# Dense and memory matmuls issued as four column tiles, and a planner that keeps GpSimd and SBUF-only DVE operations apart

## The chip, the cores and the metric

One core of one Trainium2 chip runs the whole program. The metric is device time in microseconds (us), the median of repeated executions. A profiled execution gives a trace beside it: every instruction of every engine with its start and length. The engines are PE (TensorE, matmuls; the trace lists its weight loads apart, as PEld), DVE (VectorE), ACT (ScalarE), POOL (GpSimd) and SP, which only issues DMAs here.

## What is computed

Two layers of the same kind follow each other, on 2048 tokens of 640 features, in bf16. A layer adds an attention block and then a feed-forward block to `x`, each behind a layer norm. Cut to what matters:

```python
H, Dh, N, L = 32, 20, 4, 512              # heads, width of a head, segments, tokens of a segment
def attention(x):                         # x: (1, 2048, 640)
    q, k, v = x @ wq, x @ wk, x @ wv      # split into heads and segments
    for s in range(N):
        p = softmax(q_s k_s^T * Dh**-0.5 + causal mask)
        a_dot = p v_s
        pq = phi(q_s)                     # phi(t) = t + 1 if t > 0 else exp(t)
        a_mem = (pq M) / (pq z + 1e-6)    # what the memory holds of the segments before
        o_s = g * a_mem + (1 - g) * a_dot # g = sigmoid(beta), one per head
        M, z = M + phi(k_s)^T v_s, z + sum(phi(k_s))
    return concat(o) @ wo
def feed_forward(x):
    return relu(x @ w1) @ w2              # 1728 hidden features
for layer in range(2):                    # the same weights twice
    x = x + attention(norm(x)); x = x + feed_forward(norm(x))
```

## The kernel before

**Tiling.** Work goes by layer `a` (0, 1) and segment `s` (0 to 3) of 512 tokens. The features lie in five chunks of 128 partitions. PE does these kinds of work, and the form in which it uses its array of 128 x 128 is what the change is about:

- *Dense* products, in `group` (L644 to L656): the first matmul of a group is recorded at L651, the others at L654. Query, key and first feed-forward products stream 512 columns, value, output and second feed-forward products 320. Each uses the whole array (128 rows by 128 columns).
- *Scores* (`scores`, L1114): a head is only 20 wide, so four heads sit in four strips of 32 rows and run side by side (row tiles). Keys and queries are brought into that layout by way of DRAM (`spill`, `fill`). A pair of head groups has five rounds; a round fills PSUM slots X and Y, and ACT turns each into exponentials (`exps`, L1166). There are 32 pairs, so 160 rounds. POOL zeroes what the causal mask forbids (`causal`, L1178).
- *Values* (`apply`, L1257): exponentials times values. The output of a head is 21 wide, so four heads sit in four strips of 32 columns (column tiles); 16 matmuls of 512, 384, 256 and 128 columns for one group of heads. Pairs 2 and 3 go another way, `values_by_token` (L1208): the whole array, 40 short matmuls of 21 columns at a time.
- *Memory* reads (`mem_read`, L1007) and writes (`mem_write`, L1058): the whole array, 84 to 168 columns each.
- The last 64 hidden features of the feed-forward block (`ffn_last`, L1405): two strips of 64 columns.
- Idle matmuls (`keep_busy`, L638) that the planner puts into gaps of PE.

**The order** of all instructions is worked out on the host by a planner, `Sched`. Each piece of the work is a generator (a *stream* with a priority) that yields operations (`Op`); an operation has the engines that may do it, a price in ns, the waits, and a `mode`, the form of PE: "full", "rows" or "cols". At each step the planner takes, over all streams, the operation that could start first, ties going to the lower priority. Where an operation's mode is not the one that PE is in, `switch` is added to its price (L264) and 97 ns to the time kept for it (L336). A "cols" operation that would come while PE is in "full" is held back by up to 4 us while scores remain (`JOIN_NS`, L297), so that it rather follows scores. DVE operations are priced at 66 ns plus their columns, and nothing is known to the planner of what POOL does at that time. 48 plans are made with 48 values of `switch`; the one that a replay with random DMA delays (`late`) finds shortest is emitted. The waits in the program come from the data alone, not from the planner's times.

Of the kernel before, what the change touches and what calls it, by code (L numbers as in the profile page):

```python
# [11 lines left out]
D = 640  # L12
# [101 lines left out]
class Op:  # L114
# [4 lines left out]
    def __init__(self, alts, waits, dma=None, acq=None, urgent=False, take=(), mode="full"):  # L119
        self.alts = alts  # L120
        self.mode = mode
# [4 lines left out]
        self.take = take  # L126

# [38 lines left out]
IDLE_NS = 300.0  # L166
SURE_NS = 800.0
# [9 lines left out]
class Sched:  # L177


    def __init__(self, prog, switch):  # L180
        self.P = prog
        self.switch = switch
        self.log = []
        self.free = {e: 800.0 for e in ENGS}
        self.t = {}
        self.events = {}
        self.streams = []
        self.dma_free = 0.0
        self.pe_mode = "full"
        self.spare = []  # L190
        self.idle_fn = None

    def keep_busy(self, op, start):
# [10 lines left out]
        if n > 1:  # L204
            self.log.append(("pe", 56.0 * n, 0.0, s.tks, [], False))
# [47 lines left out]

    def _alts(self, op):
# [7 lines left out]
        for k, (e, hold, fns, tail) in enumerate(op.alts):  # L262
            m = PE_MARGIN if e == "pe" else 0.0
            if e == "pe" and op.mode != self.pe_mode:  # L264
                hold = hold + self.switch
            start = max([self.at(t) + SEM_NS + m for t in waits], default=0.0)
            start = max(self.free[e], start)
            res.append((start + hold, start, k, e))
        return res

    def run(self):
        while True:
# [52 lines left out]
            e, hold, fns, tail = op.alts[k]  # L325
            waits, slot = op.waits, None
# [7 lines left out]
            if e == "pe":  # L334
                self.keep_busy(op, start)
                if op.mode != self.pe_mode:  # L336
                    hold = hold + SWITCH_NS
            self.P.waits(e, waits)
            self.free[e] = end
            if e == "pe":  # L340
                self.pe_mode = op.mode
# [15 lines left out]
            self.log.append((e, hold, tail, waits, out if isinstance(out, list) else [out], op.dma is not None))  # L357
            st[2], st[3] = None, ((slot, out) if slot is not None else out,)

    def late(self, seed):  # L360
# [5 lines left out]
        for e, hold, tail, waits, out, is_dma in self.log:  # L366
# [3 lines left out]
            if e == 'pe' and start - free[e] > 800.0 and start > 10e3:  # L370
                start += COOL_NS
            free[e] = start + hold
# [15 lines left out]
def pe(ns, fns, waits=(), acq=None, take=(), mode="full"):  # L388
    return Op([("pe", ns, fns, 190.0)], waits, acq=acq, take=take, mode=mode)
# [29 lines left out]
def plan(switch, sb, sem_, psum, dram, A_x, A_wq, A_wk, A_wv, A_wo, A_beta, B_x, B_w1, B_w2, out):  # L419
# [156 lines left out]
    def consts():  # L576
# [37 lines left out]
        ta = yield dve(32, 1, lambda e: e.tensor_scalar(gt[:, 1, :], gt[:, 0, :], 1.0, None, ALU.add), [te])  # L614
        tr = yield dve(256, 1, lambda e: e.reciprocal(gt[:, 1, :], gt[:, 1, :]), [ta])
        tg = yield dve(32, 1, lambda e: e.tensor_scalar(gt[:, 2, :], gt[:, 1, :], -1.0, 1.0, ALU.mult, ALU.add), [tr])
# [5 lines left out]
        for c in range(FC):  # L622
            h0, h1 = CH_H0[c], CH_H1[c]
            mc = maskg[:, CH_OFF[c]:CH_OFF[c + 1]].rearrange("p (h e) -> p h e", e=DH + 1)[:, :, 0:DH]
            tm = yield dve(140, 1, lambda e, mc=mc, h0=h0, h1=h1: e.tensor_tensor(
# [18 lines left out]
    def group(slots, n, mms, waits):  # L644

        bk = tk = None
        last = len(mms) - 1
        for k, (a, b, *w) in enumerate(mms):
            w = list(w[0]) if w else []
            if k == 0:  # L650
                bk, tk = yield pe(mm_ns(n), [(lambda e, bk, a=a, b=b: e.matmul(  # L651
                    bk.ap[:, 0:n] if len(b.shape) == 2 else bk.ap[:, 0:n].rearrange("p (i n) -> p i n", n=128), a, b, start=True, stop=(last == 0)), last == 0)], list(waits) + w, acq=slots)
            else:
                tk = yield pe(mm_ns(n), [(lambda e, k=k, a=a, b=b, bk=bk: e.matmul(  # L654
                    bk.ap[:, 0:n] if len(b.shape) == 2 else bk.ap[:, 0:n].rearrange("p (i n) -> p i n", n=128), a, b, start=False, stop=(k == last)), k == last)], w)
# [3 lines left out]
    def stats(t, xt):  # L659
        tk = None  # L660
        for c2 in range(2):
# [3 lines left out]
            mv[:, t, :], stats6[:, t, :, :].rearrange("p c s -> p (c s)")), [tk])  # L665
        return tk

    def chain(t0, n, tk, sq=None):

        sl = slice(t0, t0 + n)  # L670
        if sq is None:
            tk = yield dve(n, 1, lambda e: e.tensor_scalar(lnU[:, sl], mv[:, sl, 1], LN_EPS, None, ALU.add), tk)  # L672
        else:
            tk = yield dve(n, 1, lambda e: e.tensor_scalar(lnU[:, sl], sq, 1.0 / D, LN_EPS, ALU.mult, ALU.add), tk)
# [11 lines left out]
    def lnorm(s, x_tks, pool_, parts=1):  # L686
# [3 lines left out]
        for p0 in range(0, 4, n):  # L690
# [11 lines left out]
            for i in range(p0, p0 + n, 2):  # L702
# [4 lines left out]
                bx, t0 = yield dve(D, 4, lambda e, bx, t=t: nm(e, bx, t, 0), [tch], extra=120, acq=XN)  # L707
                t1 = yield dve(D, 4, lambda e, bx=bx, t=t: nm(e, bx, t, 1), [tch], extra=120)
# [6 lines left out]
    def normed(t, k, bx, tch):  # L715
        return dve(D, 4, lambda e: e.tensor_scalar(  # L716
# [236 lines left out]
    def phi_(n):  # L953
        def f(a, s):
# [6 lines left out]
            for c in range(FC):  # L961
# [5 lines left out]
                tr = yield dve(512, 4, lambda e, rt=rt, q=q: e.tensor_scalar(  # L967
# [7 lines left out]
                tp = yield dve(512, 2, lambda e, rt=rt, dst=dst: e.tensor_tensor(dst, dst, rt.ap, ALU.min),  # L975
# [18 lines left out]
    def mem_read(hb):  # L994
        def f(a, s):
# [8 lines left out]
            for i in range(NJ):  # L1004
                fns = []
                for z, (c, h0, h1) in enumerate(lst):
                    fns.append((lambda e, bk, c=c, h0=h0, h1=h1, z=z, i=i: e.matmul(  # L1007
                        bk.ap[:, (h0 - 16 * hb) * 21:(h1 - 16 * hb) * 21],
                        STGS[sx(a, s)][:, c, 1, i * 128:(i + 1) * 128],
                        BD[:, CH_OFF[c] + (h0 - CH_H0[c]) * 21:CH_OFF[c] + (h1 - CH_H0[c]) * 21],  # L1010
                        start=(z == 0), stop=True, skip_group_check=True), z == len(lst) - 1))
# [565 lines left out]
```

## Time and profile before

| | |
|---|---|
| median of 3 runs | 562.56 us (562.47 to 562.56) |
| the profiled execution | 562.46 us |
| its span, first to last instruction | 560.6 us |
| instructions in the trace | 12651, of them 5110 matmuls and 5111 weight loads |
| scores, first to last start | 19.47 to 478.80 us |

The profile names an instruction by its line in the kernel, so that L651 and L654 together are all dense products. Busy time of PE counts a matmul from its start to a modelled end; two that follow each other overlap, so the pace of PE is read from the starts. Rows of the table of windows give, for a stretch of the span, each engine's busy time and count of instructions.

### The profile page before, as it was taken

The numbers are of one execution on the slowest core, as the hardware profiler recorded it, in microseconds if no ns is written. First come the engines' busy times: TensorE is split into PE (matmuls) and PEld (weight loads), VectorE is DVE, ScalarE is ACT, GpSimd is POOL, SyncE is SP. The second block draws the span as 40 slices with busy tenths as digits, with TensorE's granted clock in tenths as the row PEclk, the third lists the DMA queues.
The fourth block names the chain that finished last, engine by engine and source line by source line (L and its number), as shares of the span: only waits on it lengthen the run. The fifth ranks groups of instructions, "written<-read, shape, count | busy, mean of one in ns | idle before, by whom it ended". The sixth has DMA issues, their size and how long they took to land.

```text
span 560.6 us, 12651 instructions
## 1 busy us (share of the span) xinstructions
PE 555.5 (99%) x5110; PEld 302.6 (54%) x5111; DVE 410.8 (73%) x1060; ACT 409.7 (73%) x522; POOL 194.3 (35%) x302
## 2 busy tenths in 40 slices
PE   8999999999999999999999999999999999999998
PEld 7654545545644455645356554465445654665655
DVE  5898899776998787877888987889824866651202
ACT  5799999987699779787897789877856788323140
POOL 4534344333354444344433443335401433100000
DMA  8599988741374137443373505550325510422101
GB/s 269 118 201 219 254 202 164 172 123 44 90 175 99 50 89 185 88 99 79 97 179 52 127 20 137 131 120 20 67 77 154 114 43 20 93 69 55 41 1 47
DMA packets 132219, 61.43 MB, mean 110 GB/s; under 512 B 111042, under 2 KB 122050, under 8 KB 132162
## 3 DMA queue, kind: packets, MB, share of 16 engines
q1 hardware_dynamic: 131942, 60.37, 45.7%
q8 instruction: 40, 0.66, 0.5%
q10 hardware_dynamic: 220, 0.26, 0.2%
q14 instruction: 17, 0.14, 0.1%
HBM read 20.57 MB, written 12.85 MB: 60 GB/s over the span
## 4 chain that ended last, share of the span: by engine, by line
PE 90%; DVE 8%; DMA 1%; ACT 0%; POOL 0%; issue 0%
PE ps L654 58%; PE ps L651 12%; PE ps L1114 9%; PE ps L1257 7%; DVE stats L662 2%; PE ps L1058 2%; PE ps L1007 2%; DVE x_sb L1328 1%; PE ps L1405 1%; DVE stg L827 1%; DMA x_sb<-in_A_x_dram 1%; DVE xn_tok L704 1%; DVE av L1265 0%; DVE xn_tok L716 0%; DVE mv L664 0%; ACT PT L1166 0%
## 5 line engine op out<-in xcount | busy, mean ns | idle before, releaser
L1166 ACT ACTIVATE PT<-ps 128x1024 bf16<-128x1024 f32 x320 | 310.1, 1022 | 66.1 <-PE ps L1114 64.5
L1178 POOL TENSOR_SCALAR_AFFINE_SELECT PT<-PT 128x512 bf16<-128x512 bf16 x256 | 166.3, 668 | 267.7 <-ACT PT L1166 267.7
L654 PE MATMUL ps<-w_r,hT 128*128 128x320 bf16 (+2 forms) x768 | 123.4, 299 | 0.1
L654 PE MATMUL ps<-xnT,w_r 128*128 128x512 bf16 x416 | 113.6, 379 | 0.0
L1328 DVE TENSOR_TENSOR x_sb<-x_sb,ps 128x320 bf16<-128x320 bf16 (+1 forms) x128 | 60.4, 479 | 70.2 <-PE ps L654 69.9
L654 PEld LDWEIGHTS ps<-w_r,hT 128*128 128x128 bf16 x768 | 72.2, 98 | 34.2 <-issue 6.3
L1436 ACT ACTIVATE hT<-ps 128x512 bf16<-128x512 f32 x55 | 33.0, 599 | 46.4 <-PE ps L654 46.1
L1114 PE MATMUL ps<-pad 20*128 20x384 bf16 (+3 forms) x1024 | 64.9, 301 | 0.0
L654 PEld LDWEIGHTS ps<-xnT,w_r 128*128 128x128 bf16 x416 | 39.7, 98 | 42.1 <-issue 2.9
L662 DVE BATCH_NORM_STATS2 stats<-x_sb 128x6 f32<-128x320 bf16 x126 | 55.9, 470 | 2.3 <-DMA x_sb<-in_A_x_dram 2.0
L1265 DVE CAST av<-ps 128x512 bf16<-128x512 f32 x56 | 38.3, 684 | 12.9 <-PE ps L1257 12.5
L1114 PEld LDWEIGHTS ps<-pad 20*128 20x128 bf16 x1024 | 18.2, 92 | 51.4 <-ACT PT L1166 24.2
L654 PE MATMUL ps<-wo_r,oT 128*128 128x320 bf16 x256 | 45.3, 299 | 0.0
L1434 DVE TENSOR_SCALAR hT<-ps 128x512 bf16<-128x512 f32 x49 | 33.5, 684 | 10.5 <-PE ps L654 10.0
L1257 PE MATMUL ps<-PT,v_aug 128*32 128x256 bf16 (+5 forms) x896 | 40.7, 302 | 0.0
L651 PE MATMUL ps<-xnT,w_r 128*128 128x512 bf16 x104 | 39.6, 381 | 0.0
L654 PE MATMUL ps<-wv_r,xnT 128*128 128x320 bf16 x192 | 35.8, 300 | 0.0
L654 PE MATMUL ps<-xnT,wk_r 128*128 128x512 bf16 (+1 forms) x140 | 35.5, 349 | 0.0
L676 POOL TENSOR_TENSOR rstd<-lnU,mhalf 128x2 f32<-128x2 f32 (+2 forms) x25 | 20.3, 811 | 39.9 <-DVE lnU L672 39.7
L654 PE MATMUL ps<-xnT,wq_r 128*128 128x512 bf16 (+1 forms) x140 | 33.9, 349 | 0.0
L1301 DVE TENSOR_TENSOR o_sb<-avt,rden 128x320 bf16<-128x320 bf16 x60 | 33.3, 572 | 0.7
L654 PEld LDWEIGHTS ps<-wo_r,oT 128*128 128x128 bf16 x256 | 24.8, 98 | 11.3 <-issue 1.3
(120 smaller groups left out, 686.9 us busy)
## 6 DMA issues: line engine op xcount, KB each, us to landing
pad<-scr SPq DMA_DIRECT2D x124, 80.0 KB
scr<-stg SPq DMA_DIRECT2D x34, 256.0 KB, 2.9
out_dram<-x_sb SPq DMA_DIRECT2D x15, 160.0 KB, 1.8
w_r<-in_B_w_dram SPq DMA_DIRECT2D x10, 216.0 KB, 3.3
w_r<-in_B_w_dram SPq DMA_DIRECT2D x13, 160.0 KB, 2.7
x_sb<-in_A_x_dram SPq DMA_DIRECT2D x9, 160.0 KB, 3.3
scr<-w_r SPq DMA_DIRECT2D x5, 256.0 KB, 3.5
x_sb<-in_A_x_dram SPq DMA_DIRECT2D x3, 320.0 KB, 7.3
```

The costliest lines, as they stand in the source:

```text
L651: bk, tk = yield pe(mm_ns(n), [(lambda e, bk, a=a, b=b: e.matmul(bk.ap[:, 0:n] if len(b.shape) == 2 else bk.ap[:, 0:n].rearrange("p (i n) ...
L654: tk = yield pe(mm_ns(n), [(lambda e, k=k, a=a, b=b, bk=bk: e.matmul(bk.ap[:, 0:n] if len(b.shape) == 2 else bk.ap[:, 0:n].rearrange("p (i ...
L662: tk = yield dve(320, 1, lambda e, c2=c2: e.bn_stats(stats6[:, t, c2, :], x_sb[:, t, c2 * 320:(c2 + 1) * 320]), xt)
L1114: fns.append([(lambda e, z=z, j=j, hh=hh, N=N, o=o, sl=sl: e.matmul(ps[:, hh, o:o + N], sl.ap[32 * hh:32 * hh + DH, z, 0, 128 * j:128 * j ...
L1166: tx = yield act(1024, lambda e, dst=dst, src=src: e.activation(dst, src, ACT.Exp, scale=SCALE), sc + pw)
L1178: tm = yield pool(600.0, lambda e, reg=reg: e.affine_select(out=reg, in_=reg, pattern=[[0, 4], [1, 128]], compare_op=ALU.is_ge, fill=0.0, ...
L1257: fns.append((lambda e, bk, j=j, hh=hh, pt=pt, g=g0 + z: e.matmul(bk.ap[32 * hh:32 * hh + wide(g, hh), 128 * j:L], VAUG[vx(a, s)][:, j].re ...
L1265: te = yield evac(L, 1, lambda e, sl=sl, z=z, bk=bk: e.tensor_copy(sl.ap[:, z], bk.ap), lambda e, sl=sl, z=z, bk=bk: e.activation(sl.ap[:, ...
L1301: to = yield dve(320, 1, lambda e, dst=dst, src=src, rz=rz: e.tensor_tensor(dst, src, rz, ALU.mult), [tg] + OSB.tks)
L1328: ta = yield dve(n, 1, lambda e: e.tensor_tensor(x_sb[:, t, c0:c0 + n], x_sb[:, t, c0:c0 + n], bk.ap[:, 0:n], ALU.add), [tk] + list(waits) ...
L1434: th = yield evac(512, 1, lambda e, dc=dc, bk=bk: e.tensor_scalar(hT[:, dc, :], bk.ap[:, :], 0.0, None, ALU.max), lambda e, dc=dc, bk=bk: ...
L1436: lambda e, dc=dc, bk=bk: e.activation(hT[:, dc, :], bk.ap[:, :], ACT.Relu), [tk] + HT.tks)
```

## The change

**Column tiles.** `pe` gets `cols`, a second list of instructions, and `cols_ns`, what they take more. `group`, `mem_read` and `mem_write` hand over such a list: each matmul of 128 output columns becomes four, with 32 columns of the weights each, that write partitions 0 to 31, 32 to 63, 64 to 95 and 96 to 127 of the same PSUM bank. The planner takes the list when PE is in "cols" or "rows" and scores remain (`mode_of`); PE is then in "cols". Behind an operation in "full" that has no such list (L1208 above all) dense work stays in "full" until the next scores, and after the last scores all of it is in "full". `ffn_last` goes from two strips of 64 columns to four of 32.

**POOL and DVE.** Operations of DVE that read and write SBUF alone, with the exception of bn_stats and a few others, are marked `shared` (`dvs` in place of `dve`), as is every POOL operation. In the planner and in its replay, one that would start while a shared operation of the other engine runs starts 140 ns before that one's end instead. No wait is added to the program. Two prices change: the mask from 600 to 635 ns, bn_aggr by +40 ns.

The diff, cut to its core:

```diff
+OTHER = {"dve": "pool", "pool": "dve"}
+OVER_NS = 140.0
...
+    def mode_of(self, op):
+        return "cols" if op.cols is not None and self.pe_mode in ("cols", "rows") and not self.streams[0][4] else op.mode
...
-            if e == "pe" and op.mode != self.pe_mode:
+            if e == "pe" and self.mode_of(op) != self.pe_mode:
                 hold = hold + self.switch
+            if e == "pe" and op.cols is not None and self.mode_of(op) != op.mode:
+                hold = hold + op.cols_ns
             start = max([self.at(t) + SEM_NS + m for t in waits], default=0.0)
             start = max(self.free[e], start)
+            if op.shared and e in OTHER:
+                a, b = self.spans[OTHER[e]]
+                if a <= start < b - OVER_NS:
+                    start = b - OVER_NS
...
+            mode = self.mode_of(op)
+            if e == "pe" and mode != op.mode:
+                fns = op.cols
...
+def dvs(n, mode, fn, waits=(), extra=0.0, acq=None, urgent=False):
+
+    op = dve(n, mode, fn, waits, extra, acq, urgent)
+    op.shared = True
+    return op
...
+            def whole(e, bk, k=k, a=a, b=b, wide=wide):
+                return e.matmul(to(bk.ap, wide), a, b, start=(k == 0), stop=(k == last))
+
+            def tile(e, bk, y, k=k, a=a, b=b, wide=wide):
+                return e.matmul(to(bk.ap[32 * y:32 * y + 32], wide), a[:, 32 * y:32 * y + 32], b,
+                                start=(k == 0), stop=(k == last))
...
-                bk, tk = yield pe(60.0 * len(lst), fns, phi + bdt, acq=MISC[:1])
+                bk, tk = yield pe(60.0 * len(lst), fns, phi + bdt, acq=MISC[:1], cols=cols, cols_ns=3.0 * len(lst))
...
-                tm = yield pool(600.0, lambda e, reg=reg: e.affine_select(
+                tm = yield pool(635.0, lambda e, reg=reg: e.affine_select(
...
             for z in range(2):
-                fns.append((lambda e, bk, k=k, z=z: e.matmul(
-                    bk.ap[64 * z:64 * z + 64, 0:256].rearrange("p (i n) -> p i n", n=128),
-                    w1_r[:, k, NFULL * 128:DFF], feat(xt, k)[:, 2 * z:2 * z + 2],
-                    start=(k == 0), stop=(k == FC - 1)), k == FC - 1 and z == 1))
+                for y in range(2):
+                    fns.append((lambda e, bk, k=k, z=z, y=y: e.matmul(
+                        bk.ap[64 * z + 32 * y:64 * z + 32 * y + 32, 0:256].rearrange("p (i n) -> p i n", n=128),
+                        w1_r[:, k, NFULL * 128 + 32 * y:NFULL * 128 + 32 * y + 32], feat(xt, k)[:, 2 * z:2 * z + 2],
+                        start=(k == 0), stop=(k == FC - 1)), k == FC - 1 and (z, y) == (1, 1)))
```

More of the change, by code (lines that the diff above doesn't have):

```diff
@@ L126, in __init__ @@
         self.take = take
+        self.shared = alts[0][0] == "pool"
 class Slot:
@@ L335, in run @@
                 self.keep_busy(op, start)
-                if op.mode != self.pe_mode:
+                if mode != self.pe_mode:
                     hold = hold + SWITCH_NS
+                if mode != op.mode:
+                    hold = hold + op.cols_ns
+            shared = op.shared and e in OTHER
+            if shared:
+                self.spans[e] = (start, end)
             self.P.waits(e, waits)
@@ L365, in late @@
         dma_free = 0.0
-        for e, hold, tail, waits, out, is_dma in self.log:
+        spans = {"pool": (0.0, 0.0), "dve": (0.0, 0.0)}
+        for e, hold, tail, waits, out, is_dma, shared in self.log:
             m = SEM_NS + (PE_MARGIN if e == "pe" else 0.0)
```

99 lines of the change are left out of this document (62 added, 37 removed).

## The prediction

> **What bounds the kernel now.** I read the page's engine totals first, then the chain that ended last.
>
> ```profile
> span 560.6 us, 12651 instructions
> PE 555.5 (99%) x5110; PEld 302.6 (54%) x5111; DVE 410.8 (73%) x1060; ACT 409.7 (73%) x522; POOL 194.3 (35%) x302
> ...
> PE 90%; DVE 8%; DMA 1%; ACT 0%; POOL 0%; issue 0%
> ```
>
> PE is busy from end to end and is 90% of the chain: it is the bound. The question is whether PE's time is all arithmetic. The table of windows, cut at the first scores, the end of the weight loads and the last scores, has three stretches behind the start (columns: window, length, then busy us and count of PE, PEld, DVE, ACT, POOL).
>
> ```profile
> 19.50:106.00 86.50, 85.96 (x909) 46.66 (x909) 80.05 (x225) 81.53 (x109) 36.52 (x54) 1.00 0.87 196
> 106.00:479.00 373.00, 372.91 (x3511) 193.12 (x3509) 294.86 (x741) 299.25 (x362) 145.41 (x221) 1.00 0.42 97
> 479.00:560.60 81.60, 79.23 (x542) 48.05 (x535) 23.88 (x58) 18.83 (x31) 2.88 (x5) 1.00 0.20 51
> ```
>
> In the middle 373 us PE is busy for 372.91, while ACT (299.25) and DVE (294.86) have a fifth of their time free: what PE saves there shortens the kernel. Between 19.5 and 106 ACT is busy 81.53 of 86.5 us and DVE 80.05, so little can be saved there. The clock column (third from the right) is 1.00 throughout.
>
> But "busy" hides something, and PE's timeline shows it (start, length to the last matmul's end, line, tile, shape of the first, count).
>
> ```profile
> 200.70 0.40 PE L1114 MATMUL ps<-pad 20*128 20x384 bf16 x8
> 201.02 0.73 PE L1257 MATMUL ps<-PT,v_aug 128*32 128x512 bf16 x16
> 201.68 0.31 PE L651 MATMUL ps<-wo_r,oT 128*128 128x320 bf16 x1
> 201.83 0.30 PE L654 MATMUL ps<-wo_r,oT 128*128 128x320 bf16 x1
> 201.97 0.33 PE L1007 MATMUL ps<-BD,stg 128*128 128x84 bf16 x3
> 202.14 0.84 PE L654 MATMUL ps<-wo_r,oT 128*128 128x320 bf16 x5
> 202.82 0.30 PE L651 MATMUL ps<-wo_r,oT 128*128 128x320 bf16 x1
> 202.95 0.57 PE L654 MATMUL ps<-wo_r,oT 128*128 128x320 bf16 x3
> 203.46 0.40 PE L1114 MATMUL ps<-pad 20*128 20x256 bf16 x8
> ```
>
> Matmuls overlap, so I go by starts. Five dense matmuls of 320 columns take 202.14 to 202.82: 0.136 us each, 0.425 ns a column. Scores (L1114) run four side by side: 384 + 128 columns are 0.218 us, but the next start comes after 0.32. Values (L1257) are 1280 columns, 0.544 us, and the next start comes after 0.66. Three dense ones should take 0.408 and the scores come after 0.51. So each change between scores (row tiles), values (column tiles) and dense work (whole array) costs 0.10 to 0.12 us with no arithmetic in it; the first matmul behind it is late too (201.68 to 201.83, 0.15 for 0.136).
>
> **How many changes.** Going down PE's rows of the timeline I count 163 stretches of scores; the first and the last:
>
> ```profile
> 19.47 0.40 PE L1114 MATMUL ps<-pad 20*128 20x512 bf16 x4
> ...
> 478.80 0.40 PE L1114 MATMUL ps<-pad 20*128 20x384 bf16 x8
> ```
>
> From 106 to 479 us there are 315 changes of form: 128 into scores (124 from dense, 4 from column work), 48 scores to values, 79 scores to dense, 52 column work to dense, 8 dense to column work. There are 80 before and 7 after.
>
> **The change, part by part.** (1) Behind scores and values, a dense or memory matmul is issued as four of 32 output columns each, in the values' form. The 52 + 8 changes between values and dense work go; scores still cost one change in and one out. An edge out of column work costs 0.116 + 0.014, one into it 0.10 + 0.014: 52 × 0.130 + 8 × 0.114 = **-7.7 us** in the middle window. The last feed-forward block (L1405) goes from two tiles of 64 to four of 32, because those two forms cost a change as well:
>
> ```profile
> 393.11 0.74 PE L1405 MATMUL ps<-xnT,w_r 128*64 128x256 bf16 x10
> 393.77 0.73 PE L1257 MATMUL ps<-PT,v_aug 128*32 128x512 bf16 x16
> 394.43 0.34 PE L1007 MATMUL ps<-BD,stg 128*128 128x147 bf16 x3
> ```
>
> 1280 columns again, 0.544, and 0.66 to the next start. It happens once: counted in the margin.
>
> (2) Leaving four column tiles for scores costs 0.116 where leaving dense work cost 0.10: the four start one behind the other. 124 such exits at 0.013: **+1.6 us**.
>
> (3) Dense in steady state. Inside a values visit four tiles run 512 + 384 + 256 + 128 columns at the dense rate, so I price the dense matmuls (L651 and L654, the window's rows by line below) at nothing: 245 + 1,353 = 1,598. One of 320 columns now needs eight instructions in 0.136 us, 17 ns each.
>
> ```profile
> 106.00:479.00 373.00, 82.67 (x245) 23.68 (x244) 1.00 0.42 97
> 106.00:479.00 373.00, 275.51 (x1353) 126.64 (x1353) 1.00 0.42 97
> ...
> 201.02 0.40 PE L1257 MATMUL ps<-PT,v_aug 128*32 128x512 bf16 x4
> ...
> 201.02 0.12 PEld L1257 LDWEIGHTS ps<-PT,v_aug 128*32 128x32 bf16 x8 [0.21 <-issue]
> ...
> 55.07 1.16 PE L1208 MATMUL ps<-w_r,PT 128*128 128x21 bf16 x40
> ```
>
> The four 512-column matmuls of a values visit are done in 0.40 us, and forty load-and-matmul pairs of L1208 start within about 1.0 us (1.16 less the length of the last), 25 ns a pair, 12.5 ns an instruction: fast enough, though for 80 instructions and not thousands. That pace is the cover; what it costs if it is missing is rival C.
>
> (4) Memory matmuls (L1007, L1058) are short: 84 to 168 columns by the code, and the three from 201.97 to 202.14 above took 0.057 us each. The window's rows by line (L1007, then L1058):
>
> ```profile
> 106.00:479.00 373.00, 13.50 (x120) 8.78 (x120) 1.00 0.42 97
> 106.00:479.00 373.00, 7.41 (x88) 5.94 (x87) 1.00 0.42 97
> ```
>
> That is 208. From above: the shortest step from four tiles to the next four is that from 256 columns to 128, 256 × 0.425 = 0.109 us, so the four loads could take up to 0.109 unseen, 0.052 more than 0.057. From below: nothing. The nearest row is that of the eight loads above: all within 0.12 us although one takes 0.097 (the median by the view of that line, below), so they start 3 ns apart and run side by side. I take 4 ns: **+0.8 us**.
>
> ```profile
> L1257 PEld LDWEIGHTS ps<-PT,v_aug x896: 87/97/98, 82.0 to 483.6; 128*32 128x32 bf16 x173, 128*21 128x21 bf16 x7
> ```
>
> (5) Before 106 us nine changes go (7 out of values, 2 in), some 1.1 us, but up to five come back, since the values of pairs 2 and 3 (L1208) stay in whole-array form. With ACT at 94% I take **-0.2**. Bounds: -2.8, if the 30 idle matmuls there (first row below, 0.056 us each, 128 columns) go as well, and +1. After 479 us the plan goes back to whole-array form: nothing.
>
> ```profile
> 19.47:106.00 86.53, 2.53 (x30) 1.74 (x30) 1.00 0.87 196
> 106.00:479.00 373.00, 1.00 (x9) 0.67 (x9) 1.00 0.42 97
> ```
>
> (6) Column values no longer wait up to 4 us in the planner to join other column work, and idle-time filler (L638), still in whole-array form, costs two unplanned changes where it falls between tiles, 0.23 us: 9 fillers in the middle window, in two or three places, **+0.5**.
>
> (7) The planner now lets a GpSimd mask and an SBUF-only DVE operation exclude each other. The trace has the effect:
>
> ```profile
> L967 DVE TENSOR_SCALAR rtmp<-stg x50: 225/282/818, 13.1 to 440.6; 128x512 bf16<-128x512 bf16 x50
> ```
>
> The same operation takes 282 ns at the median and 818 at worst. No instruction changes, only the order. What PE waits for on other engines in the whole run is this:
>
> ```profile
> PE ps L634 <- POOL mhalf L587: 1.6, 1, 1.6
> PE ps L739 <- DVE xn_tok L716: 0.6, 3, 0.2
> PE ps L1007 <- DVE om_sb L1018: 0.3, 1, 0.3
> PE ps L651 <- DVE av L1265: 0.3, 1, 0.3
> ```
>
> 2.2 of the 2.8 us lie ahead of the first scores, so a better order has under 1 us to win: 0, bounds -0.6 and +2 for an order that comes out worse.
>
> **The sum.** -7.7 + 1.6 + 0.8 - 0.2 + 0.5 = -5.0 us. The profiled execution took 562.46 (span 560.6), the median is 562.56, no different. 562.46 - 5.0 = **557.5**. Its own range: memory at 0, (5) and (7) at their best give -9.0, 553.5; memory at a quarter of its upper end (+1.9) and (5) at its worst (+1.2) give 560.6, and (7) at its worst alone, 559.5, lies inside.
>
> **Rivals.** *B, the short groups starve* (slower). If the four loads of a memory matmul run one after the other, each takes 0.109 instead of 0.057: 208 × 0.052 = +10.8 in place of +0.8, so 557.5 + 10.0 = **567.5**. It decides from 5.8 / 208 = 28 ns a matmul on. For it: no row has two four-tile groups of under 128 columns in a row. Against it: the loads' starts. The Trainium skill has a rule on this side: "TensorEngine Tiling (Array Packing)", Feature Incompatibilities, says that column tiling excludes Fast Weight Load, and "TensorE: Matmul & The Clock Gate", LDWEIGHTS, gives a load its columns over 1.2 in ns; an estimate from it, if four loads go in sequence, is 4 × 27 = 107 ns a group, which would put this case at 557.5 - 0.8 + 208 × 0.050 = 567.1. The eight loads within 0.12 us speak against a sequence.
>
> *C, dense groups can't be issued in time* (slower). PE's instructions grow from 10,221 by six for each tiled matmul, some 13,000. Of a segment's dense matmuls 192 of 307 have 320 columns by the code, so 1,000 of the 1,598, with 17 ns an instruction; at 20 ns one takes 0.160, and all cost 1,000 × 0.024 = +24, **581**. It decides from 5 ns a group on. Against it: the 12.5 ns of L1208. They are fetched by DMA, too, and that queue has room (packets, MB, share of the DMA engines):
>
> ```profile
> q8 instruction: 40, 0.66, 0.5%
> ```
>
> Forty fetches of 16 KB become some 90, and 0.5% of the DMA time some 1.2%.
>
> *D, the gain isn't collected.* ACT paces the scores and PE fills up with idle matmuls or waits. For it: ACT is at 94% up to 106 us. Against: 80% behind it. If three quarters of the gain go, 562.46 - 1.25 = **561.2**; if all, 562.5. That dense work stays in whole-array form, the change doing nothing, ends there as well.
>
> **How the numbers follow.** Forecast 0.70, B 0.12, C 0.04, D 0.14. 0.2% of 562.56 is 1.1 us, about what a measurement of this kernel can tell from no change: faster is below 561.4. Faster: 0.69 of the forecast and 0.08 of D, 0.77; same: 0.06 of D and 0.02 of a mild B, 0.08; slower: the rest of B and C, 0.15. The range 553.5 to 562.6 leaves out B and C but for a mild B, and the forecast's far end, under 2 in 10.
>
> **What would show it.** Right: about 255 changes of form between the first steady window and the last scores where 315 were; dense groups of four at 0.136 and 0.216 us; memory groups near 0.065. Wrong: memory groups at 0.1 (B), dense ones of 320 columns above 0.14 (C), more filler or PE waits behind ACT and DVE (D). A changed order that adds stretches of scores beyond 163 would undo the sum at 0.24 us each.

## The result, and the profile after

The changed kernel takes **568.82 us** (median of 4 runs, 568.12 to 570.78) against 562.51 (562.25 to 562.56) for the kernel before beside it: 1.012 times as long, 95% interval 1.0109 to 1.0132. The forecast was 557.5 with a range to 562.6. It missed, on the other side; the time lies just beyond rival B's 567.5, but by another cause. By the medians the kernel is 6.3 us slower. The profiled execution, from which the views below come, was the longest of the four: 570.78 us (span 568.9), 8.32 more than that of before.

Page of the kernel after: span, engine totals, the queue of instruction fetches (packets, MB, share of the DMA engines), shares of the chain that ended last.

```profile
span 568.9 us, 26024 instructions
PE 553.3 (97%) x11782; PEld 322.9 (57%) x11782; DVE 404.6 (71%) x1049; ACT 415.1 (73%) x533; POOL 195.7 (34%) x302
...
q8 instruction: 92, 1.51, 1.1%
...
PE 73%; DMA 13%; DVE 9%; ACT 3%; SPq 1%; issue 1%; POOL 0%; DVEq 0%; ACTq 0%
```

PE went from 10,221 instructions to 23,564, and the fetches from 40 to 92. The chain had 90% PE and 1% DMA; now it has 73% and 13%: PE does less and waits for transfers. The windows of the kernel after (the same columns as in the prediction) say where.

```profile
19.50:106.00 86.50, 84.43 (x1987) 48.61 (x1986) 76.69 (x219) 78.41 (x102) 37.25 (x55) 1.00 0.97 194
106.00:479.00 373.00, 364.20 (x8845) 207.07 (x8845) 284.29 (x724) 301.01 (x373) 141.99 (x214) 1.00 0.49 99
479.00:568.90 89.90, 87.58 (x793) 52.56 (x785) 29.81 (x68) 27.14 (x41) 7.23 (x12) 1.00 0.22 51
```

In the middle PE stood idle for 0.09 us of 373 before; it is 8.80 now. What ended the longest of PE's waits after (us in total, times, longest):

```profile
PE ps L1117 <- DMA phk<-phs: 2.8, 2, 2.2
...
PE ps L1058 <- DVE om_sb L1075: 1.2, 2, 0.8
PE ps L1181 <- DMA pad<-scr: 1.1, 1, 1.1
PE ps L696 <- DMA oT<-o_sb: 1.1, 1, 1.1
PE ps L696 <- DVE av L1332: 1.1, 1, 1.1
```

Of these the list before had only `om_sb` and `av`, with 0.3 us each. Three name DMAs, two of them DMA transposes (`phk`, `oT`); DVE, named in the two others, waits for transposes itself (below, under e4).

**A ledger of PE's time.** To split "busy" I give every matmul or group of four tiles its columns at 0.417 ns plus 2.4 ns, and look at what lies between two starts beyond that: up to 0.125 us at a change of form is its price, up to 0.04 elsewhere is small change, and the rest is waiting. (By this count before has 317 changes in the middle, where the prediction counted 315.) Sums in us, in the profiled executions:

```
                  changes of form    base   in changes  small  waits  total
before                405            505.6     40.9      6.8    3.2   556.5
after                 342            506.9     35.9      6.4   15.6   564.8
difference            -63             +1.3     -5.0     -0.4  +12.4    +8.3
106 to 479 before     317                      32.0             0.3
106 to 479 after      248                      26.0            11.1
```

So the gain that was forecast is there, and waiting took it back more than twice over. The pace of the tiled work stands in PE's timeline after:

```profile
201.07 0.39 PE L696 MATMUL ps<-xnT,w_r 128*32 128x512 bf16 x4
201.29 0.35 PE L1058 MATMUL ps<-BD,stg 128*32 128x84 bf16 x12
201.46 0.39 PE L696 MATMUL ps<-xnT,w_r 128*32 128x512 bf16 x4
201.78 0.40 PE L1181 MATMUL ps<-pad 20*128 20x384 bf16 x8
202.11 1.26 PE L696 MATMUL ps<-xnT,w_r 128*32 128x512 bf16 x20
203.20 0.35 PE L1058 MATMUL ps<-BD,stg 128*32 128x84 bf16 x12
```

Three memory groups take 0.17 us (201.29 to 201.46), 0.057 each, what three whole ones took; five dense groups of 512 take 1.09 (202.11 to 203.20), 0.218 each. By their starts in the whole run (medians) a group of 84 columns takes 0.039 us, one of 147 0.067 and one of 320 0.136; whole matmuls before took 0.040, 0.067 and 0.136. Between memory and dense work there is no pause. Four tiles cost PE nothing here.

**One wait followed back.** The longest, 2.2 us ahead of L1117: PE's rows in the timeline of all engines, SP's own timeline, and the piece of the chain (start, us).

```profile
228.19 0.72 PE L1324 MATMUL ps<-PT,v_aug 128*32 128x512 bf16 x16
...
231.07 1.30 PE L1117 MATMUL ps<-v_aug,phk 128*32 128x147 bf16 x36 [2.17 <-DMA phk<-phs]
...
232.30 0.61 PE L1181 MATMUL ps<-pad 20*128 20x384 bf16 x8
```

```profile
225.41 1.45 SPq L731 DMA_TRANSPOSE phk<-phs  x1
226.96 1.90 SPq L994 DMA_DIRECT2D pad<-scr  x4
228.90 1.45 SPq L949 DMA_DIRECT2D scr<-stg  x2
```

```profile
225.41 5.62 DMA phk<-phs
```

The transpose is issued at 225.41 and lands at 231.03. In the DMA records its last packet of 256 bytes ends at 229.01, and landing follows 2.02 us later. In the kernel before, 74 of the 88 transposes meet no fetch from their first packet to their landing, and there landing follows the last packet by 0.55 us in the mean. Here a fetch of instructions runs from 229.00 to 229.97.

### The profile page after: what moved, and what is told of

Read it like the earlier page. It is cut to its first block, busy times and chain, and to the rows that moved or that the text cites. A ratio compares the mean times of both kernels' runs of the same rounds, so it can differ in the third digit from the quotient of the medians.

```text
span 568.9 us, 26024 instructions
## 1 busy us (share of the span) xinstructions
PE 553.3 (97%) x11782; PEld 322.9 (57%) x11782; DVE 404.6 (71%) x1049; ACT 415.1 (73%) x533; POOL 195.7 (34%) x302
## 4 chain that ended last, share of the span: by engine, by line
PE 73%; DMA 13%; DVE 9%; ACT 3%; SPq 1%; issue 1%; POOL 0%; DVEq 0%; ACTq 0%
PE ps L696 42%; PE ps L693 15%; DMA avt<-av 8%; PE ps L1181 7%; PE ps L1324 4%; DMA phk<-phs 2%; ACT PT L1233 2%; DVE stats L711 2%; PE ps L1117 2%; DVE x_sb L1395 1%; PE ps L1058 1%; DVE o_sb L1368 1%; DMA xnT<-xn_tok 1%; DVE av L1332 1%; DMA pad<-scr 1%; DMA scr<-w_r 1%
## 5 line engine op out<-in xcount | busy, mean ns | idle before, releaser
L696 PE MATMUL ps<-xnT,w_r 128*32 128x512 bf16 x1560 | 101.3, 380 | 0.1
L696 PE MATMUL ps<-w_r,hT 128*32 128x320 bf16 x2220 | 93.6, 301 | 0.0
L696 PEld LDWEIGHTS ps<-w_r,hT 128*32 128x32 bf16 x2220 | 55.9, 97 | 21.7 <-issue 6.8
L1181 PE MATMUL ps<-pad 20*128 20x512 bf16 (+3 forms) x1024 | 65.8, 302 | 2.1 <-DMA pad<-scr 1.1
L696 PEld LDWEIGHTS ps<-xnT,w_r 128*32 128x32 bf16 x1560 | 37.7, 96 | 34.1 <-issue 6.1
L696 PE MATMUL ps<-wo_r,oT 128*32 128x320 bf16 x1120 | 46.0, 300 | 1.1 <-DMA oT<-o_sb 1.1
L693 PE MATMUL ps<-w_r,hT 128*128 128x320 bf16 (+2 forms) x277 | 40.9, 299 | 0.0
L696 PE MATMUL ps<-xnT,wk_r 128*32 128x512 bf16 (+1 forms) x580 | 38.8, 365 | 1.6 <-DVE av L1332 1.1
L696 PE MATMUL ps<-wv_r,xnT 128*32 128x320 bf16 x860 | 39.1, 300 | 0.9 <-DMA xnT<-xn_tok 0.9
L696 PE MATMUL ps<-xnT,wq_r 128*32 128x512 bf16 (+1 forms) x592 | 37.4, 363 | 0.0
```

The lines of the kernel that those rows point to most:

```text
L693: return e.matmul(to(bk.ap, wide), a, b, start=(k == 0), stop=(k == last))
L696: return e.matmul(to(bk.ap[32 * y:32 * y + 32], wide), a[:, 32 * y:32 * y + 32], b, start=(k == 0), stop=(k == last))
L1181: fns.append([(lambda e, z=z, j=j, hh=hh, N=N, o=o, sl=sl: e.matmul(ps[:, hh, o:o + N], sl.ap[32 * hh:32 * hh + DH, z, 0, 128 * j:128 * j ...
```

## The experiments

**Theory F, the fetches:** more PE instructions mean more fetches; a transpose in flight that meets one lands later; PE works in the order planned, so it waits. **Rival O:** the new order of POOL and DVE, or the order that the tiles give the planner, makes the waits. The first expectations count *bursts*: runs of 256-byte packets less than 0.6 us apart, at least 100 of them. By that count 13 of 58 bursts meet a fetch before and 38 of 58 after, and the longest packet of a burst that meets one lasts 1.4 us at the median after, 0.02 in the others. Later I matched the 88 transposes one by one; the column "met" counts those whose packets overlap a fetch.

| kernel | median us | ratio to before (95%) | fetches | met | waits, us (106 to 479) | changes |
|---|---|---|---|---|---|---|
| before | 562.5 | | 40 | 14 | 3.2 (0.3) | 405 |
| after | 568.82 | 1.012 (1.0109 to 1.0132) | 92 | 42 | 15.6 (11.1) | 342 |
| e1 | 566.9 | 1.0088 (1.0048 to 1.0127) | 92 | 38 | 10.5 (7.9) | 347 |
| e2 | 565.61 | 1.0052 (1.0037 to 1.0067) | 41 | 14 | 1.2 (0.0) | 408 |
| e3 | 569.36 | 1.0119 (1.0104 to 1.0134) | 41 | 18 | 5.3 (1.9) | 451 |
| e4 | 568.69 | 1.0107 (1.0092 to 1.0122) | 92 | 48 | 13.1 (9.9) | 346 |
| f1 | 563.23 | 1.0008 (0.9986 to 1.0029) | 91 | 44 | 7.2 (4.0) | 343 |
| f2 | 563.59 | 1.0016 (1.0007 to 1.0025) | 58 | 28 | 11.1 (6.9) | 337 |
| f3 | 559.0 | 0.9934 (0.9919 to 0.9949) | 60 | 24 | 5.0 (2.0) | 337 |
| f4 | 565.9 | 1.0059 (1.0045 to 1.0073) | 40 | 17 | 3.3 (0.2) | 410 |
| f5 | 561.21 | 0.9977 (0.9966 to 0.9988) | 60 | 24 | 9.7 (4.7) | 336 |
| e5 | 570.62 | 1.0136 (1.0119 to 1.0153) | 60 | 24 | 5.6 (0.6) | 405 |
| e6 | 574.33 | 1.0215 (1.0192 to 1.0237) | 96 | 48 | 12.1 (6.6) | 346 |
| e7 | 588.14 | 1.0455 (1.0437 to 1.0472) | 99 | 37 | 8.8 (3.6) | 405 |

**e1: the tiles without the part on POOL and DVE.**

```diff
-    op.shared = True
+    op.shared = False
...
-                tm = yield pool(635.0, lambda e, reg=reg: e.affine_select(
+                tm = yield pool(600.0, lambda e, reg=reg: e.affine_select(
```

> Column tiles alone: GpSimd and DVE are planned as before the change (no exclusion, mask at 600 ns, bn_aggr without its 40). Theory F (fetch): the tiles more than double PE's instructions, their 16 KB fetches hit DMA transposes in flight, these land some 1.5 us late and PE, in order, waits. By it the time stays where the changed kernel is, 565 to 571 us, with PE waits of 10 us or more and over 30 of the 58 bursts of transposes meeting a fetch. Theory O (order): the new planning of GpSimd and DVE puts PE's work into a worse order. By it 557 to 559 us, with PE waits of 3 to 4 us as before the change.

566.9 us, widely spread (564.08 to 571.9 in 6 runs), with 92 fetches and 10.5 us of waits. The tiles alone make the kernel slower; its interval overlaps that of the whole change, so what the other part adds to it is not told apart.

**e2: the part on POOL and DVE without the tiles.**

```diff
-        return "cols" if op.cols is not None and self.pe_mode in ("cols", "rows") and not self.streams[0][4] else op.mode
+        return op.mode
...
```

> The planning of GpSimd and DVE alone; every matmul in the form it had before, the last feed-forward block in two strips of 64. Theory F: 561 to 564 us, some 40 fetches, some 13 of 58 bursts of transposes hit, PE waits of 3 to 5 us. Theory O: PE waits of over 10 us and 570 us or more, since the some 60 changes of form between values and dense work are back as well.

565.61 us, between what the two expectations gave (561 to 564, and 570 or more): that order costs some 3 us by itself, but not through waits, which fall to 1.2. The groups by line of e2, then of before, have the idle matmuls that the planner puts into gaps:

```profile
L674 PE MATMUL ps<-ident 128*128 128x128 bf16 x130 | 9.3, 224 | 0.2 <-DVE xnT L794 0.2
```

```profile
L638 PE MATMUL ps<-ident 128*128 128x128 bf16 x54 | 5.0, 231 | 0.1
```

76 more at 0.056 us are +4.3, less 2.0 of waits: +2.3 of the 3. The plan has POOL and DVE exclude each other, expects gaps, and fills them; whether PE would have waited there without the filler, no run shows. With the tiles the same part adds no filler (x54 after), so this price is not a term of the whole change.

**e3: the plan of after, every matmul issued whole.**

```diff
-            if e == "pe" and mode != op.mode:
-                fns = op.cols
```

> The order of the changed kernel, instruction for instruction on ACT, DVE, GpSimd and SP, but each dense and memory matmul is issued as one on the whole array. Changes of form go back from 342 to some 410, +7 us. Theory F: fetches go back to some 40, hit bursts of transposes from 38 to some 13 of 58, PE waits from 15.6 us to some 4, so 562 to 566 us. Theory O: the waits stay at 12 us or more and the time is 573 to 577 us.

569.36 us: the time lies between the two expectations and meets neither. It is nearly that of after, but it is made up differently. The order was planned for tiles; issued whole it has 451 changes of form, not 410, and 45.7 us in changes against 35.9 after. Waits, with 41 fetches, fall to 5.3 from 15.6, near the 4 that F gave. So this order costs changes, and not the waits.

**e4: the plan of before, tiles put in as the instructions are written out.** The planning is that of before in every step.

```diff
+            if e == "pe":
+                self.form = "cols" if op.cols is not None and self.form in ("cols", "rows") and not self.streams[0][4] else op.mode
+                if self.form != op.mode:
+                    fns = op.cols
...
```

> The order of the kernel before, but dense and memory matmuls behind scores and values are issued as four tiles of 32 columns wherever the changed kernel's rule would do so, the last feed-forward block in four strips of 32. Changes of form fall from 405 to some 345, -6 us. Theory F: some 92 fetches, over 30 of 58 bursts of transposes hit, PE waits rise from 3 us to 8 to 15, so 562 to 570 us. Theory O: waits stay at 3 to 4 us and the time is 556 to 558 us.

568.69 us, with 92 fetches and 13.1 us of waits. **The order of before, which had 3.2 us of waits, has 13.1 when its matmuls are tiles.** So the waits need no new order, which is against O. The two longest sums among PE's waits in e4 are for transposes; neither is in the list of before:

```profile
PE ps L1120 <- DMA phk<-phs: 3.3, 3, 1.4
PE ps L699 <- DMA xnT<-xn_tok: 2.0, 2, 1.8
```

The transposes `avt` in the view of that tile, first before: for how long DVE waited for them (us, times), and issue to landing.

```profile
  DMA avt<-av: 1.8, 4
...
DMA to landing us min/median/max: 2.7/2.8/5.0
```

The same view of e4:

```profile
  DMA avt<-av: 14.6, 12
...
DMA to landing us min/median/max: 2.7/3.8/6.7
```

Both issue the same 88 transposes in the same order, so each can be set beside its twin. For those of which the trace has a landing in both, the table has the change in us of the time from issue to landing. Here a transpose counts as meeting a fetch if one runs between its first packet and its landing, so there are more of them than under "met" above (51 in place of 37 in e7):

```
                           newly meet a fetch             meet none in either
before to e4 (tiles)       35: mean +1.05, max +3.29      22: mean +0.27, median +0.02
before to e7 (quarters)    44: mean +0.92, max +2.14      26: mean +0.10, median +0.01
before to f2 (few tiles)   26: mean +1.12, max +2.09      48: mean +0.11, median +0.01
e3 to after                24: mean +0.73, max +2.13      17: mean +0.09, median +0.01
```

The three in e4 that no longer meet a fetch land 1.11 us earlier. Of the +1.05, 0.31 lies between the last packet and the landing, the rest ahead of it. A few are late without a fetch of their own (5 of the 22 in e4 by over 0.5 us); these the runs don't explain.

**m1: transposes beside nothing, whole matmuls, tiles, and short whole matmuls.** 88 transposes of 128 x 1280 one after the other; PE idle for 16 of them, then the three kinds of matmul in turn.

```diff
+                for n in range(400):
+                    for y in range(4):
+                        e.matmul(ps[32 * y:32 * y + 32, 1, :], w[:, 32 * y:32 * y + 32], mov[:], start=True, stop=True)
+                for n in range(400):
+                    for y in range(4):
+                        e.matmul(ps[:, 2, 128 * y:128 * y + 128], w[:], mov[:, 128 * y:128 * y + 128], start=True, stop=True)
```

> Computes none of the reference: SP issues 88 DMA transposes of the kernel's size one behind the other, while PE does nothing (16 transposes), then 400 whole-array matmuls of 512 columns, then the same as 1600 column tiles of 32, then as 1600 whole-array matmuls of 128 columns; the output is zeros. Theory F (fetch): a transpose takes 1 to 2 us longer when an instruction fetch falls into it, and not otherwise; fetches come some four times as often in both stretches with 1600 matmuls, so both have some 40 to 60% of their transposes hit, the stretch with 400 some 10 to 15%, and tiles do not matter. Theory P (port): four tiles read SBUF four times over and slow the transposes down themselves; then the stretch of column tiles has longer transposes even without a fetch, and the 1600 narrow whole-array matmuls do not.

The transposes' tile view of m1 in the stretches with PE idle, with whole matmuls, with tiles and with short whole ones (issue to landing):

```profile
DMA to landing us min/median/max: 3.3/3.3/3.4
...
DMA to landing us min/median/max: 3.3/3.3/4.5
...
DMA to landing us min/median/max: 3.3/3.3/5.1
...
DMA to landing us min/median/max: 3.3/3.4/4.3
```

Without a fetch, transposes follow each other every 3.36 us in all four stretches: what PE does is nothing to them. With one it is 4.01 (3 of whole), 3.66 (14 of tiles) and 3.86 (10 of short). The shares that meet one are as F gave them, but they are 0.3 to 0.65 us later, and not 1 to 2: a fetch costs a transpose less here than the 1 us in the kernel, and why isn't shown. Tiles and short matmuls, with the same number of instructions, behave alike. 400 groups of four tiles took 86.1 us and 400 whole matmuls 87.4; the 1.3 between them lie in the first seven whole matmuls, which start the stretch at half the pace (see the clock, below).

**f1, f2, f3: mending.** If F holds, a plan that expects transposes later, or fewer tiles, must win some of it back. f1 is e1 with 1.4 us more for each transpose in the plan; f2 has the order of before and tiles only between two visits of scores that also hold column work and nothing that must be whole; f3 is both.

```diff
+        lat = lat + 1400.0
...
+        for k, span in enumerate(spans):
+            if k and any(r[0].mode == "cols" for r in span) and not any(
+                    r[0].mode == "full" and r[0].cols is None for r in span):
+                for op, at, n, slot, more in span:
+                    if op.cols is not None and more:
+                        swap[at] = (n, op, slot)
```

> Column tiles alone, with the planner told that a DMA transpose lands 1.4 us later than it thought. The program still has some 91 fetches and over 25 hit bursts. Theory F: PE's waits fall from 10.5 us to 3 to 6, since what is late is now expected to be late, and the time to 557 to 562 us. If the waits have another cause than late transposes, they stay at 9 us or more and the time is 564 to 570 us.

> The order of the kernel before again, but a dense or memory matmul becomes four tiles only where its stretch between two visits of scores holds values or the last feed-forward block: elsewhere entering and leaving the whole-array form costs no more than the tiles' form. 7,444 matmuls instead of 5,110 (before) and 11,731 (tiles everywhere), so some 58 fetches. Changes of form some 350. Theory F: hit bursts of transposes between 13 and 39, some 22, PE waits 5 to 8 us (3.2 before, 13.1 with tiles everywhere), so 559 to 563 us. If what costs is the tiled form itself and not the number of instructions, waits stay near 13 us and the time is 566 us or more.

> Both together: the plan of the run with late transposes, tiles only in the stretches that hold column work (7,667 matmuls, some 60 fetches). Theory F: PE waits of 2 to 4 us, changes of form some 350, 555 to 559 us, faster than the kernel before. If late transposes are not the cause, 564 us or more.

f1 563.23 and f2 563.59: no difference from before to speak of, and both above F's ranges (557 to 562, 559 to 563). In f1 44 of 88 transposes meet a fetch, about as many as after (42) or in e1 (38), yet waits are 7.2, where e1 has 10.5 and F gave 3 to 6: the later times in the plan absorb part of the lateness. In f2 waits are still 11.1, nearer to the 13 of the expectation against F than to its 5 to 8. **f3 takes 559.0 (558.89 to 559.5), 0.9934 times before: 0.7% faster, with an interval clear of 1, and faster than the whole change.** Its page, its window and its two longest waits:

```profile
span 557.1 us, 17788 instructions
PE 550.8 (99%) x7667; PEld 311.7 (56%) x7667; DVE 404.4 (73%) x1048; ACT 415.5 (75%) x534; POOL 193.8 (35%) x302
...
q8 instruction: 60, 0.98, 0.7%
```

```profile
106.00:479.00 373.00, 371.84 (x5887) 203.25 (x5884) 292.29 (x739) 307.82 (x378) 144.34 (x221) 1.00 0.46 100
```

```profile
PE ps L704 <- POOL mhalf L657: 1.6, 1, 1.6
PE ps L1216 <- DMA pad<-scr: 0.5, 1, 0.5
```

PE's idle time in the middle is 1.16 us; it was 8.80 after. The time is at the upper end of the 555 to 559 that F gave, and the waits, 5.0, are more than its 2 to 4.

**f4 and f5: each half of f3 alone.** f4 is the kernel before with the 1.4 us in the plan; f5 is f3 without them.

> The kernel before with nothing but the planner's 1.4 us more for a DMA transpose; no tiles. It tells whether the 559.0 us of sparse tiles with late transposes comes from the tiles or from the more careful plan. Theory F: some 40 fetches, changes of form some 405 as before, PE waits of 2 to 3 us, so 561 to 564 us. If the careful plan alone made the gain: 558 to 560 us.

> Sparse tiles without the planner's 1.4 us: the plan of column tiles alone (566.9 us, 10.5 us of PE waits), tiles only in stretches that hold column work, some 60 fetches. Theory F: waits fall with the number of fetches, to 5 to 8 us, so 560 to 564 us. If the plan and not the fetches made the waits: 10 us and 566 us or more.

f4: 565.9, slower than before and than either expectation (561 to 564, 558 to 560), with 122 idle matmuls where before has 97 and the waits unchanged. So f3's gain isn't that of a more careful plan as such: that costs where there is nothing to absorb. f5: 561.21, inside F's 560 to 564, but with 9.7 us of waits where F gave 5 to 8. From f5 to f3 the same 1.4 us win 2.2.

**e5 and e7: more instructions and no tiles.** The order of before; each dense matmul as two (e5) or four (e7) whole-array matmuls over a half or a quarter of its columns.

```diff
-                bk, tk = yield pe(mm_ns(n), [(lambda e, bk, a=a, b=b: e.matmul(
...
+                bk, tk = yield pe(mm_ns(n), [
+                    (lambda e, bk, a=a, b=b, h=h: part(e, bk, a, b, h, 0), last == 0 and h == 3) for h in range(4)], list(waits) + w, acq=slots)
```

> The kernel before in its own order and forms, no column tiles, but each dense matmul is issued as two whole-array matmuls of half the columns: some 2,570 matmuls and weight loads more, some 60 fetches instead of 40. By itself this costs the 2.4 ns that each matmul takes beside its columns, 2,570 times, +6 us. Theory F (the number of instructions counts, not their form): transposes that meet a fetch rise from 14 of 88 to some 28, as with sparse tiles (58 fetches, 11.1 us of PE waits), and PE waits from 3 us to 7 to 12, so 572 to 578 us. If the tiled form is what delays PE: waits stay at 3 to 4 us and the time is 568 to 570 us.

> The kernel before in its own order, no column tiles; each dense matmul is four whole-array matmuls of a quarter of the columns, so PE has about as many instructions as with tiles everywhere and 100 fetches or a few less. By itself this costs 2.4 ns for each of the some 7,700 matmuls more, 18.5 us, so 581 us without waits beyond those of before. Theory F (the number of instructions counts, not their form): over 40 of the 88 transposes meet a fetch (48 with tiles everywhere), over 15 are more than 1 us later than in the kernel before (25 with tiles), and PE waits are 8 to 13 us, so 586 to 592 us. If column tiles are needed for the waits: some 3 to 6 us of waits, 580 to 584 us.

e5 took 570.62, between F's 572 to 578 and the 568 to 570 of the other expectation: waits rose by only 2.4. e7 took 588.14, inside F's range, with its 8.8 us of waits; 37 of its transposes meet a fetch, where F gave over 40. Both are long because the base is: short whole matmuls cost 6.3 and 18.8 us more by the ledger. Beside that, e7 at 99 fetches has 8.8 us of waits. Its fetches on the page and its DMA waits of PE:

```profile
q8 instruction: 99, 1.62, 1.2%
```

```profile
PE ps L1070 <- DMA phk<-phs: 1.4, 2, 1.0
...
PE ps L658 <- DMA oT<-o_sb: 0.8, 1, 0.8
```

PE waits for transposes of the same tiles, without a single dense one of its own in tiles, though its waits are 4.3 us less than e4's in all.

**e6: is it that PE has run ahead?** The saved changes may have been cover for the transposes, too: with them gone PE comes sooner to what it has to wait for. e4 with eight idle column-tile matmuls ahead of each values visit gives that time back.

```diff
+            pad_ = [(lambda e, bk, y=y: e.matmul(
+                bk.ap[32 * y:32 * y + 32, 0:128], ident[:, 32 * y:32 * y + 32], ident[:], start=True, stop=True), False)
+                for r in range(2) for y in range(4)]
+            bk, tk = yield pe(545.0, pad_ + fns, mk + vt, acq=MISC, mode="cols")
```

> The order of the kernel before with tiles everywhere (568.69 us, 13.1 us of PE waits, 92 fetches), and ahead of each of the 60 values visits two groups of four idle column tiles of 128 columns, 0.112 us, which give PE back about the time that one change of form took there. The two theories left: late transposes alone (F) make the waits, or they do so because the removed changes were also PE's cover for the transposes (C). F alone: the waits stay at 9 to 13 us and the time is 568.7 + 6.7 less a little, 573 to 576 us. C: with the cover back the waits fall by half or more, to 6 us or less, though as many transposes meet a fetch, and the time stays at 567 to 570 us.

574.33 us: 5.6 more than e4, with waits of 12.1 against 13.1, as F alone says. In the middle they do fall, from 9.9 to 6.6, so PE's running ahead seems to have a part in it, but giving the time back costs more than it saves.

## Why the prediction was wrong

**Where the parts stood.**
- *Changes of form* (1, 2). Right, in count and in price: some 255 forecast in the middle, 248 found; 32.0 us became 26.0, -6.0 where -7.7 + 1.6 = -6.1 was written.
- *Dense at nothing* (3) and *memory* (4). Right and on the safe side: 0.218 us for 512 columns, 0.057 for the memory groups, so the +0.8 of (4) was 0. Rivals B and C fall: groups of 84 columns follow each other every 39 ns. The 107 ns that the prediction estimated for four loads in sequence, from the Trainium skill, "TensorE: Matmul & The Clock Gate", LDWEIGHTS, are not seen. The Trainium skill's rule in "TensorEngine Tiling (Array Packing)", Key Properties, that different tiles can load and multiply in parallel, is what the trace bears out.
- *Filler* (6). The +0.5 didn't come: 97 idle matmuls before and after.
- *The stretch to 106 us* (5). One change was saved there (80 to 79), and waits rose by 1.7 (1.2 to 2.9): +1.6 instead of -0.2.
- *The order* (7). Alone it costs 3 us (e2), beyond its bound of +2, and by filler, which the prediction didn't look at. In the whole change this filler isn't there.

**The step that failed** is the one on the fetches, under rival C: "They are fetched by DMA, too, and that queue has room", with 0.5% of the DMA time becoming some 1.2%. The count was right (92 came), and the share too (1.1%). A share of 16 engines' time isn't the price, though. A fetch is one 16 KB packet of 0.9 to 1.9 us (median 1.0 in the trace of after), and a transpose in flight that newly meets one lands 0.7 to 1.1 us later in the mean, 3.3 at most. With 92 fetches in place of 40, 42 of 88 transposes met one instead of 14. The Trainium skill, "Runtime: NRT & Kernel Launch", Instruction fetch mechanics, calls the cost of crossing a 16 KiB boundary mostly hidden. For the engine that fetches, m1 agrees (400 groups of tiles in 86.1 us, 400 whole matmuls in 87.4); for the transfers that meet the fetch, these runs show a cost. The step was charged nothing, and waits grew by 12.4 us; the forecast -5.0 became +8.3 in the profiled execution, +6.3 by the medians. Not all of the 12.4 is the fetches alone: e7, with 99 of them and no change of form saved, waits 5.6 us more than before, and e4, with 92 and the changes saved, 9.9; and part of the 12.4 is the lowered clock behind one wait (last section).

The second half of the same step: the waits of before (2.8 us in the list) were read as "a better order has under 1 us to win", and a worse one was bounded at +2. That list shows how tightly the plan fits, not how much room it has: PE was idle for 0.09 us in 373. A kernel without waits has much to lose by a transfer that comes 1 us later.

**What is shown and what is open.** Shown: transposes that newly meet a fetch land 0.7 to 1.1 us later in the mean, and those that meet none are unchanged at the median (four matched pairs of kernels; m1 agrees, with less); waits rise with the order unchanged (e4), and without tiles when there are as many fetches (e7); and a plan that expects transposes later wins a part of it back (f1), with fewer tiles most (f3). Open: tiles at 92 fetches wait for 13.1 us, quarters at 99 for 8.8, and few tiles at 58 for 11.1, so the waits are no function of the count alone; which transposes are hit and how far PE has run ahead (e6) may matter, and the runs don't weigh these against each other. Each of these sums comes from one execution, and with tiles everywhere executions differ by more than before (f1: 560.44 to 566.87 us). Open, too, is why the whole change stands 1.9 us above e1, with overlapping intervals.

## What to carry to other kernels

Splitting a matmul into tiles was free for PE here but multiplied its instructions, and instructions come in by DMA: count the fetches, and ask which small-packet transfers on the critical path they will meet. In a kernel whose order is planned in advance, price a disturbance by what waits behind the transfer that it delays, and never by its share of the bandwidth. Use the split only where it saves a change, and tell the planner of the delay: f3, with both, took 559.0 us where neither the whole change (568.8) nor either half alone (563.2 with the delay, 561.2 with few tiles) came near.

## What the runs showed of the hardware

**A fetch can hold back the completion of a transpose as well as its packets.** From the end of its last packet to its landing a transpose takes 0.47 us in m1 (63 without a fetch, at most 0.49) and 0.55 in the kernel before; the one in m1 that a fetch met there took 2.02, and the three in the kernel before 2.04 in the mean. It isn't so each time: over the traces of all fifteen kernels, landing came more than 1.5 us behind the last packet in 92 of the 184 transposes with a fetch in the 0.45 us behind that packet, and in 6 of the 1,047 without.

**Four tiles of 32 columns keep the pace of the whole array** down to 84 columns, 0.039 us a group (0.040 for a whole matmul before): eight instructions, four loads and four matmuls, in 39 ns.

**The clock was lowered behind the longest wait of PE.** The windows of after around the wait at 231 us (the third column from the right is the granted clock):

```profile
228.00:231.00 3.00, 0.90 (x28) 0.45 (x20) 2.23 (x6) 1.55 (x3) 0.63 (x1) 1.00 0.96 238
231.00:233.00 2.00, 1.93 (x52) 1.27 (x56) 0.00 (x0) 0.05 (x1) 0.00 (x0) 0.54 1.11 272
233.00:236.00 3.00, 3.00 (x72) 1.98 (x64) 2.49 (x6) 1.89 (x2) 1.04 (x2) 0.73 0.61 136
236.00:240.00 4.00, 4.00 (x128) 2.75 (x128) 3.06 (x9) 2.75 (x3) 1.65 (x3) 1.00 0.01 4
```

The 0.54 and 0.73 are means over their windows: in the trace's clock records the clock is halved from 231.18 to 234.59 us, 3.41 us in all. PE's starts agree: dense groups of 320 columns follow each other every 0.267 us from 233.20 on, and every 0.136 us from 234.71 on. Half the clock for 3.41 us is 1.7 us less work, nearly as much again as the wait of 2.2 itself; the ledger has it in waits and small change. It is one case: the longest waits of e4 (1.8 us, at 167.8) and e6 (1.5) left the clock at 1.00, and no run shows how long a wait must be. The column alone doesn't tell all, either: in m1, behind 61.9 us without a matmul, the whole matmuls of 512 columns start 0.427 us apart from 62.3 to 64.4 us and 0.216 from 64.7 on, while the column says 1.00 there.
